# Sharing the PSUM banks on demand in an attention-plus-feed-forward kernel

## The chip, the cores and the metric

The kernel runs on one core of one Trainium2 chip. The metric is the device time in microseconds (us) of one execution. Before the change the median of four runs was 231.82 us (231.75 to 232.29).

The change has five parts: all eight PSUM banks are handed out on demand, singly or as pairs; both score blocks of a tile are computed in one run; two tiles are loaded at once on two queues; matmuls on zeros fill early idle time of TensorE; and the last output tile is finished in two column parts.

## The reference

Attention over 4 batches, 8 heads, 768 positions and head size 64 comes first, with a local window of 96 positions and 8 global positions. Its output, 3072 tokens of 512 values, goes through a feed-forward layer with 2048 hidden values.

```python
scores = scale * np.matmul(q, k.transpose(0, 1, 3, 2))
rel = pos[:, None] - pos[None, :]
keep = (pos[None, :] < n_global) | ((rel >= 0) & (rel < n_local))
scores = np.where(keep, scores + bias, -1e9)     # bias = -slope[head] * distance
a = softmax(scores)                              # cut: written out in the reference
x = np.matmul(a, v)  # -> (B*S, H*D)             # cut: heads put side by side
h = x @ w_in                                     # 512 -> 2048
out = (h - np.tanh(h)) @ w_out                   # 2048 -> 512
```

## The kernel before

The 3072 tokens are 24 tiles of 128. For each tile the kernel does the following:

1. It transposes k and q, computes the score block of its own 128 keys and the block of the previous 128 keys (S), takes the exponential (E), multiplies by a mask (M), multiplies by v (AV) and divides by the sum (R). The result x is transposed.
2. It projects x with `w_in` (m1). The result of 512 columns stands in one PSUM bank. ScalarE takes its tanh (th) and VectorE subtracts (g = h - tanh h). The bank is then free.
3. It multiplies g by `w_out` (m2) into one bank, which ScalarE copies out (ot) for the store.

From the fifth tile on, m1 takes two tiles at once. The first six tiles are transposed by TensorE, the later ones by DMA. A planner in the kernel's own Python simulates the engines with fixed durations. From that it decides the order of operations on each engine and which buffer each one gets. It puts no waits into the program: these are added when the program is built, from what each instruction reads and writes.

The kernel lays out PSUM as eight banks of 512 fp32 columns (its `BANK = 512`). Before the change they were split for good: two double banks for attention, four single ones for m1, m2 and the transposes.

```python
    bufs["pair"] = [psum.tile([P, 2, BANK], FP32, name=f"pair{i}") for i in range(2)]
    pl.pool("pair", 2)
    bufs["bank"] = [psum.tile([P, BANK], FP32, name=f"bank{i}") for i in range(4)]
    pl.pool("bank", 4)
    # ... cut ...
    def m1(g, f0):
        n, per = shape1(g)
        t = buf("bank", ("h", g, f0))
        xt = buf(xname(g), ("xT", g))
        for f in range(f0, f0 + per):
            j, fo = f // FJ, (f % FJ) * P
            for c in range(CD):
                nc.tensor.matmul(
                    t[:, (f - f0) * n : (f - f0 + 1) * n], w_in_bf[j][:, c, fo : fo + P], xt[:, c, 0:n],
                    start=(c == 0), stop=(c == CD - 1),
                )

    def m1_g(g, f0):
        t, th = buf("bank", ("h", g, f0)), buf("th", ("th", g, f0))
        # ... cut: g <- t - th, one VectorE instruction of 512 columns ...

    def m2(g, t, qq):
        o = buf("bank", ("o", u))
        # ... cut: four matmuls of 512 columns into o ...

    T_LD, T_W, T_ST, T_TR = 1.1, 3.15, 0.8, 0.7     # planned DMA times
    # ... cut ...
        for o in (0, 1) if i else (0,):
            pl.op(("S", u, o), PE, 0.24, lambda e, u=u, o=o: a_S(u, o),
                  # ... cut ...
                  take=[("pair", ("S", u, o)), ("po" if o else "pd", ("p", u, o))], mode="half")
            pl.op(("E", u, o), ACT, 0.97, lambda e, u=u, o=o: a_E(u, o), after=[("S", u, o)], give=[("S", u, o)])
```

`take` asks the planner for a buffer and `give` returns it. The operation `S` takes a double bank and `E` gives it back. `m1` takes a single bank and `g` gives it back.

The softmax here doesn't subtract the row's maximum and nothing guards it: scores larger than these inputs give would overflow.

## Time and profile before

The engines are PE (TensorE matmuls), PEld (its weight loads), DVE (VectorE), ACT (ScalarE), POOL (GpSimd) and SP. A profile names a group of instructions by its source line, and the lines moved with the change:

| what | before | after | its time in the profile before |
|---|---|---|---|
| score matmuls S | L282 | L317 | |
| projection m1, 8 matmuls of 256 columns | L340 | L375 | 0.87 us for 8 |
| tanh th (ACT) | L504 | L571 | 0.60 us |
| subtraction g (DVE) | L349 | L384 | 0.69 us |
| output matmuls m2, 4 of 512 columns | L359 | L418 | 0.86 us for 4 |
| copy of the output ot (ACT) | L270 | L305 | 0.58 us |

From the page of the kernel before, here are the span, the engine table, two rows of the 40 slices (busy tenths of TensorE, and its granted clock in tenths), the chain that ended last, and three groups. A group's columns are: count | busy us, mean ns of one | idle us before them, what ended most of it.

```profile
span 228.0 us, 5127 instructions
...
PE 207.8 (91%) x2056; PEld 143.3 (63%) x2056; DVE 128.1 (56%) x250; ACT 120.1 (53%) x192; POOL 71.4 (31%) x96
...
PE   1669699789999589999999999999999999999993
...
PEclk9999999999999959999999999999999999999999
...
PE 87%; DMA 4%; DVE 3%; POOL 2%; ACT 1%; issue 1%; POOLq 0%
PE bank L340 39%; PE bank L359 36%; PE pair L282 5%; PE pair L300 3%; DMA xT<-x 2%; PE pair L302 2%; PE bank L327 2%; DMA qb<-in_q_dram 2%; DVE x L312 1%; DVE pd L291 1%; ACT pd L286 0%; ACT po L286 0%; POOL vb L423 0%; POOL kb L423 0%; DVE xT L272 0%
...
L340 PE MATMUL bank<-xT,w_in_bf 128*128 128x256 bf16 (+1 forms) x896 | 100.1, 263 | 0.2 <-DMA xT<-x 0.2
L359 PE MATMUL bank<-w_out_bf,g 128*128 128x512 bf16 x384 | 95.2, 379 | 0.0
L349 DVE TENSOR_TENSOR g<-bank,th 128x512 bf16<-128x512 f32 x96 | 65.4, 689 | 50.5 <-ACT th L504 50.4
...
```

TensorE is busy 91% of the span and makes up 87% of the chain, so it is the bound. The `0.2` and `0.0` behind the two feed-forward groups say that TensorE almost never stood idle just before a feed-forward matmul. The idle time lies elsewhere. The stretches view gives it by time. Its columns are the stretch and its length, then busy us and instruction count of PE, PEld, DVE, ACT and POOL, then the granted clock, the DMA share and GB/s.

```profile
...
core 0: us, PE busy (x) PEld busy (x) DVE busy (x) ACT busy (x) POOL busy (x), PEclk, DMA share, GB/s
...
21.00:25.00 4.00, 2.00 (x42) 1.72 (x40) 2.91 (x5) 2.11 (x3) 1.41 (x2) 1.00 1.25 205
...
42.00:49.00 7.00, 4.80 (x54) 2.55 (x53) 3.83 (x8) 2.10 (x3) 4.66 (x6) 1.00 2.30 148
...
75.00:81.00 6.00, 2.83 (x48) 1.99 (x48) 4.19 (x11) 3.25 (x5) 3.50 (x4) 0.81 1.34 135
81.00:87.00 6.00, 5.94 (x47) 4.44 (x47) 2.94 (x5) 2.66 (x4) 1.69 (x2) 0.62 1.14 111
87.00:215.00 128.00, 128.00 (x1207) 88.22 (x1205) 78.39 (x142) 73.21 (x109) 21.96 (x26) 1.00 0.90 99
...
```

Up to 87 us there are holes: 2 us of 4 idle at 21 to 25, 2.2 of 7 at 42 to 49, and 3.2 of 6 at 75 to 81, after which the clock is lower. From 87 to 215 us TensorE is busy 128.00 of 128.00 us. What a piece of steady work costs shows in the chain of waits (start us, us, what):

```profile
...
204.49 0.87 PE bank L340 x8
205.37 0.86 PE bank L359 x4
206.23 0.87 PE bank L340 x8
...
```

### The profile page before, as it was taken

Reading aid. Unit: us, or ns where it says so; the run is one execution under the profiler, and the core shown is the slowest. Engines: PE = TensorE matmul, PEld = TensorE weight load, DVE = VectorE, ACT = ScalarE, POOL = GpSimd, SP = SyncE. Lnnn points to the kernel's source line nnn. Section 1 sums busy time; section 2 is a strip of 40 time slices with the busy share of each in tenths; the row PEclk is TensorE's granted clock in tenths of the full one; section 3 lists DMA queues with packets and bytes.
Section 4 is the critical chain, followed back from the end, with each engine's and each line's share of the span. In section 5 each row is a group of like instructions: output and inputs, shape, how many; then the busy total and the mean of one; then the engine's idle time right before and its main releaser. Section 6 shows DMA issues by size and latency. Waiting matters only on the chain.

```text
span 228.0 us, 5127 instructions
## 1 busy us (share of the span) xinstructions
PE 207.8 (91%) x2056; PEld 143.3 (63%) x2056; DVE 128.1 (56%) x250; ACT 120.1 (53%) x192; POOL 71.4 (31%) x96
## 2 busy tenths in 40 slices
PE   1669699789999589999999999999999999999993
PEld 0449698444864368676676676776667676666641
DVE  2565788530585748977675665576567553443310
ACT  5348466421676456666566466557546645443421
POOL 8996456531833514454314421400000000000000
PEclk9999999999999959999999999999999999999999
DMA  5999999999999999999999999793422321001112
GB/s 101 131 162 201 184 196 195 164 144 220 164 172 145 169 135 90 103 154 152 155 108 167 154 129 141 105 128 71 118 70 53 64 69 47 32 15 49 47 46 92
DMA packets 111959, 27.60 MB, mean 121 GB/s; under 512 B 104768, under 2 KB 108864, under 8 KB 111936
## 3 DMA queue, kind: packets, MB, share of 16 engines
q0 software_dynamic: 77024, 13.37, 83.5%
q1 hardware_dynamic: 34912, 13.90, 31.8%
q8 instruction: 16, 0.26, 0.5%
q14 instruction: 7, 0.06, 0.1%
HBM read 27.26 MB, written 6.29 MB: 147 GB/s over the span
## 4 chain that ended last, share of the span: by engine, by line
PE 87%; DMA 4%; DVE 3%; POOL 2%; ACT 1%; issue 1%; POOLq 0%
PE bank L340 39%; PE bank L359 36%; PE pair L282 5%; PE pair L300 3%; DMA xT<-x 2%; PE pair L302 2%; PE bank L327 2%; DMA qb<-in_q_dram 2%; DVE x L312 1%; DVE pd L291 1%; ACT pd L286 0%; ACT po L286 0%; POOL vb L423 0%; POOL kb L423 0%; DVE xT L272 0%
## 5 line engine op out<-in xcount | busy, mean ns | idle before, releaser
L340 PE MATMUL bank<-xT,w_in_bf 128*128 128x256 bf16 (+1 forms) x896 | 100.1, 263 | 0.2 <-DMA xT<-x 0.2
L359 PE MATMUL bank<-w_out_bf,g 128*128 128x512 bf16 x384 | 95.2, 379 | 0.0
L349 DVE TENSOR_TENSOR g<-bank,th 128x512 bf16<-128x512 f32 x96 | 65.4, 689 | 50.5 <-ACT th L504 50.4
L340 PEld LDWEIGHTS <-w_in_bf 128*128 128x128 bf16 x896 | 77.7, 101 | 18.8 <-issue 0.4
L504 ACT ACTIVATE th<-bank 128x512 f32<-128x512 f32 x96 | 56.9, 600 | 59.1 <-PE bank L340 58.9
L359 PEld LDWEIGHTS <-g 128*128 128x128 bf16 x384 | 36.4, 98 | 29.8
L423 POOL DMA_DIRECT2D kb<-in_k_dram x23 | 20.6, 894 | 50.9 <-DMA qT<-qb 24.9
L286 ACT ACTIVATE pd<-pair 128x1024 bf16<-128x1024 f32 x24 | 24.5, 1022 | 18.0 <-PE pair L282 17.9
L423 POOL DMA_DIRECT2D vb<-in_v_dram x24 | 21.5, 897 | 11.1 <-PE pair L282 5.1
L270 ACT COPY ot<-bank 128x512 f32<-128x512 f32 x24 | 14.0, 585 | 19.6 <-PE bank L359 19.6
L423 POOL DMA_DIRECT2D qb<-in_q_dram x23 | 20.4, 886 | 12.5 <-DMA qT<-qb 5.9
L291 DVE TENSOR_TENSOR pd<-pd,mk 128x1024 bf16<-128x1024 bf16 x24 | 16.6, 691 | 12.6 <-ACT pd L286 12.5
L286 ACT ACTIVATE po<-pair 128x1024 bf16<-128x1024 f32 x20 | 20.4, 1022 | 1.3 <-PE pair L282 1.1
L300 PE MATMUL pair<-vb,pd 128*128 128x65 bf16 x192 | 15.0, 200 | 4.6 <-DVE pd L291 4.5
L282 PE MATMUL pair<-qT,kT 64*128 64x128 bf16 x352 | 16.3, 227 | 2.4 <-DVE x L312 1.3
L300 PEld LDWEIGHTS <-pd 128*128 128x128 bf16 x192 | 12.9, 101 | 7.9 <-DVE pd L291 6.2
L282 PEld LDWEIGHTS <-kT 64*128 64x128 bf16 x352 | 10.9, 98 | 10.4 <-issue 9.4
L291 DVE TENSOR_TENSOR po<-po,mk 128x1024 bf16<-128x1024 bf16 x20 | 13.8, 692 | 6.0 <-ACT po L286 6.0
L312 DVE TENSOR_TENSOR x<-pair,rden 128x512 bf16<-128x512 f32 x24 | 16.6, 692 | 0.8
L302 PE MATMUL pair<-vb,po 128*128 128x65 bf16 x160 | 12.5, 194 | 1.6 <-DVE po L291 1.6
L302 PEld LDWEIGHTS <-po 128*128 128x128 bf16 x160 | 10.4, 97 | 3.5 <-DVE po L291 1.8
L327 PE MATMUL bank<-ident,kb 128*128 128x128 bf16 x24 | 3.3, 280 | 5.2 <-DVE kb L272 4.7
(29 smaller groups left out, 51.4 us busy)
## 6 DMA issues: line engine op xcount, KB each, us to landing
out_dram<-ot SPq DMA_DIRECT2D x24, 256.0 KB, 2.2
vb<-in_v_dram POOLq DMA_DIRECT2D x24, 128.0 KB, 6.2
kb<-in_k_dram POOLq DMA_DIRECT2D x23, 128.0 KB, 5.4
qb<-in_q_dram POOLq DMA_DIRECT2D x23, 128.0 KB, 6.0
w_in_bf<-in_moe_w_in_dram POOLq DMA_DIRECT2D x4, 512.0 KB, 10.4
w_out_bf<-in_moe_w_out_dram POOLq DMA_DIRECT2D x4, 512.0 KB, 12.9
kT<-kb SPq DMA_TRANSPOSE x18, 4.4
qT<-qb SPq DMA_TRANSPOSE x18, 4.0
```

What stands on the lines that cost most here:

```text
L270: nc.scalar.copy(out=dst, in_=src)
L282: nc.tensor.matmul(t[:, slot(2 * p + hh), :], kt[r, p, :], qt[r, p, :], start=True, stop=True)
L286: nc.scalar.activation(buf("po" if o else "pd", ("p", u, o)), t, AF.Exp, bias=0.0, scale=scale)
L291: nc.vector.tensor_tensor(out=p, in0=p, in1=mk[:, m, :, :], op=ALU.mult)
L300: nc.tensor.matmul(o, pd[:, slot(h), :], vd[:, h, :], start=True, stop=w is None)
L302: nc.tensor.matmul(o, buf("po", ("p", u, 1))[:, slot(h), :], bufs[vname(w)][got["vb", w]][:, h, :], start=False, stop=True,)
L312: nc.vector.tensor_tensor(out=x, in0=t[:, :, :, 0:Dh], in1=rd.to_broadcast([P, 2, NP, Dh]), op=ALU.mult,)
L340: nc.tensor.matmul(t[:, (f - f0) * n : (f - f0 + 1) * n], w_in_bf[j][:, c, fo : fo + P], xt[:, c, 0:n], start=(c == 0), stop=(c == CD - 1),)
L349: nc.vector.tensor_tensor(out=dst, in0=t.rearrange("q (b n) -> q b n", n=n), in1=th.rearrange("q (b n) -> q b n", n=n), op=ALU.subtract,)
L359: nc.tensor.matmul(o, gg[:, f, t * P : (t + 1) * P], w_out_bf[f // FJ][:, f % FJ, :], start=(f == 0), stop=(f == CF - 1),)
L423: pl.op(key, POOL, 0.75, lambda e, u=u, src=src, dst=dst: nc.gpsimd.dma_start(out=dst(), in_=rows(src, u)), after=[prev and ("issue", prev ...
L504: pl.op(("th", g, f), ACT, 0.55, lambda e, g=g, f=f: nc.scalar.activation(buf("th", ("th", g, f)), buf("bank", ("h", g, f)), AF.Tanh, bias ...
```

## The change

The intent: with a fixed split, attention may hold only two double banks, even when single banks are free. If any neighbouring free pair can serve as a double bank and any free bank as a single one, attention can run ahead of the feed-forward part, and both score blocks can be computed together. The other parts shorten the start and the end. The diff, cut to its core:

```diff
+    zeros = cpool.tile([P, 2 * P], BF16, name="zeros")
-    bufs["pair"] = [psum.tile([P, 2, BANK], FP32, name=f"pair{i}") for i in range(2)]
-    pl.pool("pair", 2)
-    bufs["bank"] = [psum.tile([P, BANK], FP32, name=f"bank{i}") for i in range(4)]
-    pl.pool("bank", 4)
+    pairs = [psum.tile([P, 2, BANK], FP32, name=f"pair{i}") for i in range(4)]
+    bufs["pair"] = {2 * i: t for i, t in enumerate(pairs)}
+    bufs["bank"] = [pairs[i // 2][:, i % 2, :] for i in range(8)]
 # ... in the planner; a bank in use has the time "never" (infinity) ...
+        def pick(size, free_banks, now):
+            best = None
+            if size == 2:
+                for i in range(0, 8, 2):
+                    t = max(free_banks[i], free_banks[i + 1])
+                    c = (max(t, now), -t, i)
+                    best = c if best is None or c < best else best
+            else:
+                for i in range(8):
+                    t = free_banks[i]
+                    c = (max(t, now), -max(t, free_banks[i ^ 1]), i)
+                    best = c if best is None or c < best else best
+            return best
 # ... loads, planned DMA times, masks ...
-    hw_loads = {0}
+    hw_loads = {0, 1}
-    T_LD, T_W, T_ST, T_TR = 1.1, 3.15, 0.8, 0.7
+    T_LD, T_W, T_ST, T_TR = 0.87, 2.4, 0.7, 0.5
+    DIST_AFTER = [("ld", "v", 1), ("in", 0), ("in", 1)]   # mask builds issued behind these
-                pl.op(("T", nm, u), SP, 0.6,               # DMA transposes, also those of x
+                pl.op(("T", nm, u), SP, 1.25,
 # ... scores ...
-            pl.op(("S", u, o), PE, 0.24, lambda e, u=u, o=o: a_S(u, o),
+        pl.op(("S", u), PE, 0.24 * len(os_), lambda e, u=u, os_=os_: [a_S(u, o) for o in os_],
+              take=[("pair", ("S", u, o)) for o in os_] + ...
 # ... zeros ...
+    def warm(e=None):
+        nc.tensor.matmul(buf("bank", "warm")[:, 0 : 2 * P], zeros[:, 0:P], zeros, start=True, stop=True)
+            if eng is PE and last is not None and "warm" in tags:
+                for _ in range(int((t - last - 0.15) / (0.22 if last < 8.0 else 0.15))):
+                    warm()
 # ... last tile in columns 0 to 383 and 384 to 511: m2_cols, ev_cols, store_cols, cut ...
```

A single bank is now one half of a two-bank tile. And `pick` sorts single banks by the *negative* of the time at which the bank beside them comes free. Of the banks free now, it therefore prefers one whose neighbour is in use, to keep whole pairs free for the scores.

More of the change, by code (lines that the diff above doesn't have):

```diff
@@ L39, in run @@
         avail = {n: [(0.0, i) for i in range(c)] for n, c in self.pools.items()}
+        banks = [0.0] * 8
         held = {}
@@ L48, in run @@
         order = []
+        never = float("inf")
+        def pick(size, free_banks, now):
[11 more added lines that the diff above has]
+            return best
         def ready(key):
@@ L53, in ready @@
             for a in o["after"]:
-                if a[0] == "issue":
-                    d = start.get(a[1])
-                else:
-                    d = done.get(a)
+                d = start.get(a[1]) if a[0] == "issue" else done.get(a)
                 if d is None:
@@ L60, in ready @@
                 t = max(t, d)
-            for p in o["take"]:
-                if not avail[p[0]]:
-                    return None
-                t = max(t, min(avail[p[0]])[0])
+            fb = None
+            for name, _ in o["take"]:
+                if name in ("bank", "pair"):
+                    fb = list(banks) if fb is None else fb
+                    size = 2 if name == "pair" else 1
+                    c = pick(size, fb, t)
+                    if c[0] == never:
+                        return None
+                    t = max(t, c[0])
+                    for i in range(c[2], c[2] + size):
+                        fb[i] = never
+                else:
+                    if not avail[name]:
+                        return None
+                    t = max(t, min(avail[name])[0])
             return t
@@ L88, in run @@
                     f"{k} {[a for a in ops[k]['after'] if (start.get(a[1]) if a[0] == 'issue' else done.get(a)) is None]}"
-                    f"{[p for p, _ in ops[k]['take'] if not avail[p]]}" for k in todo))
+                    f"{[p for p, _ in ops[k]['take'] if p in avail and not avail[p]]}" for k in todo))
             _, key, t, eng, us = best
@@ L92, in run @@
             end = t + us
+            if eng is PE:
+                end += 0.1 if mode and o["mode"] != mode else 0.0
+                mode = o["mode"]
             free[eng] = end
             start[key] = t
-            if eng is PE:
-                end += 0.1 if mode and o["mode"] != mode else 0.0
-                free[eng] = end
-                mode = o["mode"]
             if o["dma"]:
-                d0 = max(dma_free, end + (1.0 if eng is SP else 1.3))
+                d0 = max(dma_free, end + 1.2)
                 dma_free = d0 + o["dma"]
@@ L107, in run @@
             got = {}
+            now = t
             for name, tag in o["take"]:
-                b = min(avail[name])
-                avail[name].remove(b)
-                held[tag] = (name, b[1])
+                if name in ("bank", "pair"):
+                    size = 2 if name == "pair" else 1
+                    i = pick(size, banks, now)[2]
+                    for x in range(i, i + size):
+                        banks[x] = never
+                    held[tag] = (name, i)
+                else:
+                    b = min(avail[name])
+                    avail[name].remove(b)
+                    held[tag] = (name, b[1])
             for tag in o["give"]:
                 name, i = held.pop(tag)
-                avail[name].append((done[key], i))
+                if name in ("bank", "pair"):
+                    for x in range(i, i + (2 if name == "pair" else 1)):
+                        banks[x] = done[key]
+                else:
+                    avail[name].append((done[key], i))
                 got[tag] = i
-            for tag in list(held):
+            for tag in held:
                 got[tag] = held[tag][1]
@@ L185 @@
     w_out_bf = [cpool.tile([P, FJ, DM], BF16, name=f"w_out_bf{j}") for j in range(WJ)]
-    sb("kf", [P, H, Dh], FP32, 2)
+    sb("kf", [P, H, Dh], FP32, 4)
     sb("kb", [P, H * Dh], BF16, 4)
@@ L352, in m1_g, with m2_cols, ev_cols, store_cols @@
         )
+    SPLIT = 384
+    def m2_cols(u, part, qs):
+        g = group_of[u]
+        t = groups[g].index(u)
+        c0, c1 = (0, SPLIT) if part == 0 else (SPLIT, DM)
+        o = buf("bank", ("o", u, part))
+        gg = buf(gname(g), ("g", g))
+        for f in qs:
+            nc.tensor.matmul(
+                o[:, 0 : c1 - c0], gg[:, f, t * P : (t + 1) * P], w_out_bf[f // FJ][:, f % FJ, c0:c1],
+                start=(f == 0), stop=(f == CF - 1),
+            )
+    def ev_cols(e, u, part):
+        c0, c1 = (0, SPLIT) if part == 0 else (SPLIT, DM)
+        copy(e, buf("ot", ("ot", u))[:, c0:c1], buf("bank", ("o", u, part))[:, 0 : c1 - c0])
+    def store_cols(u, part):
+        b, i = tiles[u]
+        r = (b * NQ + i) * P
+        c0, c1 = (0, SPLIT) if part == 0 else (SPLIT, DM)
+        nc.sync.dma_start(out=out[r : r + P, c0:c1], in_=buf("ot", ("ot", u))[:, c0:c1])
     def m2(g, t, qq):
@@ L383 @@
     for m in range(3):
-        pl.op(("dist", m), POOL, 2.0 if m == 0 else 1.2, lambda e, m=m: build_dist(m), pri=-2 if m == 0 else 1)
+        pl.op(("dist", m), POOL, 2.0 if m == 0 else 1.2, lambda e, m=m: build_dist(m),
+              after=[("issue", DIST_AFTER[m])], pri=-2 if m == 0 else -1.5)
         for half in range(2):
@@ L418 @@
                           take=[("kf", ("kf", nm, u))], dma=T_LD)
-                    pl.op(key, DVE, 0.43, lambda e, u=u, nm=nm, dst=dst: copy(e, dst(), buf("kf", ("kf", nm, u))),
+                    pl.op(key, [(DVE, 0.43), (ACT, 0.6)], None,
+                          lambda e, u=u, nm=nm, dst=dst: copy(e, dst(), buf("kf", ("kf", nm, u))),
                           after=[("ldf", nm, u)], take=take, give=[("kf", nm, u)])
@@ L422 @@
                     go = [kk for a, kk in prog if a <= u - AHEAD - 1.5] if u >= 6 else []
-                    pl.op(key, POOL, 0.75, lambda e, u=u, src=src, dst=dst: nc.gpsimd.dma_start(out=dst(), in_=rows(src, u)),
+                    pl.op(key, POOL, 0.88, lambda e, u=u, src=src, dst=dst: nc.gpsimd.dma_start(out=dst(), in_=rows(src, u)),
                           after=[prev and ("issue", prev), go[-1] if go else None], take=take, dma=T_LD,
@@ L452 @@
         Te = (lambda nm, u: ("Te", nm, u) if u < NPE else ("T", nm, u))
-        for o in (0, 1) if i else (0,):
-            pl.op(("S", u, o), PE, 0.24, lambda e, u=u, o=o: a_S(u, o),
-                  after=[Te("k", u), Te("q", u), ("K", w) if o and tiles[w][1] else None, go,
-                         ("issue", ("S", u, 0)) if o else None],
-                  take=[("pair", ("S", u, o)), ("po" if o else "pd", ("p", u, o))],
-                  give=([("qT", u)] if o == (1 if i else 0) else []) + ([("kT", w)] if o and tiles[w][1] else []), mode="half")
-            pl.op(("E", u, o), ACT, 0.97, lambda e, u=u, o=o: a_E(u, o), after=[("S", u, o)], give=[("S", u, o)])
+        os_ = (0, 1) if i else (0,)
+        pl.op(("S", u), PE, 0.24 * len(os_), lambda e, u=u, os_=os_: [a_S(u, o) for o in os_],
+              after=[Te("k", u), Te("q", u), ("K", w) if i >= 2 else None, go],
+              take=[("pair", ("S", u, o)) for o in os_] + [("po" if o else "pd", ("p", u, o)) for o in os_],
+              give=[("qT", u)] + ([("kT", w)] if i >= 2 else []) + ([("kT", u)] if i == NQ - 1 else []), mode="half")
+        for o in os_:
+            pl.op(("E", u, o), ACT, 0.97, lambda e, u=u, o=o: a_E(u, o),
+                  after=[("S", u), ("issue", ("E", u, 0)) if o else None], give=[("S", u, o)])
             pl.op(("M", u, o), DVE, 0.7, lambda e, u=u, o=o: a_M(u, o),
                   after=[("E", u, o)] + [("mk", 2 if o else min(i, 1), half) for half in range(2)])
-        if i == NQ - 1:
-            pl.ops["S", u, 0]["give"].append(("kT", u))
         if 1 <= i < NQ - 1:
-            pl.op(("K", u), DVE, 0.2, lambda e, u=u: a_K(u), after=[("S", u, 0)])
+            pl.op(("K", u), DVE, 0.2, lambda e, u=u: a_K(u), after=[("S", u)])
             pl.op(("V", u), DVE, 0.25, lambda e, u=u: a_V(u), after=[("AV", u), ("ld", "v", b)])
@@ L488 @@
         else:
-            pl.op(("X", u), SP, 0.6,
+            pl.op(("X", u), SP, 1.25,
                   lambda e, u=u, g=g, off=off: nc.sync.dma_start_transpose(
@@ L492 @@
                   after=[("R", u), ("issue", prevx) if prevx else None], take=xt, give=[("x", u)], dma=T_TR, lag=0.5, pri=-1)
+    def warm(e=None):
+        nc.tensor.matmul(buf("bank", "warm")[:, 0 : 2 * P], zeros[:, 0:P], zeros, start=True, stop=True)
+    pl.op(("zero",), DVE, 0.1, lambda e: nc.vector.memset(zeros, 0.0), pri=-4)
+    pl.op(("warm",), PE, 0.2, warm, after=[("zero",)], take=[("bank", "warm")], pri=-4, mode="full")
+    pl.ops["S", HEAD - 1]["give"].append("warm")
     pl.op(("vone",), DVE, 0.6, lambda e: [nc.vector.memset(t[:, :, Dh : Dh + 1], 1.0) for t in bufs["vb"] + bufs["vb0_"]], pri=-3)
@@ L509 @@
         for t, u in enumerate(us):
+            if u == NU - 1:
+                for qq in range(4):
+                    pl.op(("m2", g, t, qq), PE, 0.65,
+                          lambda e, u=u, qq=qq: m2_cols(u, 0, range(qq * 4, qq * 4 + 4)),
+                          after=[("out", qq), ("g", g, (4 * qq + 3) // per * per)],
+                          take=[("bank", ("o", u, 0)), ("bank", ("o", u, 1)), ("acc", ("acc", u))] if qq == 0 else [],
+                          pri=2, mode="full")
+                pl.op(("m2", g, t, 4), PE, 0.9, lambda e, u=u: m2_cols(u, 1, range(CF)), after=[("issue", ("m2", g, t, 3))],
+                      give=[("g", g), ("acc", u)], pri=2, mode="full")
+                for part in range(2):
+                    pl.op(("ev", u, part), [(ACT, 0.45 if part == 0 else 0.25), (DVE, 0.5 if part == 0 else 0.26)], None,
+                          lambda e, u=u, part=part: ev_cols(e, u, part), after=[("m2", g, t, 3 + part)],
+                          take=[("ot", ("ot", u))] if part == 0 else [], give=[("o", u, part)], pri=1)
+                    pl.op(("st", u, part), SP, 0.4, lambda e, u=u, part=part: store_cols(u, part),
+                          after=[("ev", u, part)], give=[("ot", u)] if part else [], dma=0.5 if part == 0 else 0.3)
+                continue
             for qq in range(4):
@@ L520 @@
         [kk for a, kk in prog if kk[1] >= HEAD],
-        [("m2", g, t, qq) for g, us in enumerate(groups) for t in range(len(us)) for qq in range(4) if g >= HEAD],
+        [("m2", g, t, qq) for g, us in enumerate(groups) for t in range(len(us)) for qq in range(4) if g >= HEAD]
+        + [("m2", len(groups) - 1, 1, 4)],
     ]
@@ L532 @@
     with tc.manual_schedule(engines={PE, ACT, DVE, POOL, SP}):
+        last = None
         for t, n, key, eng, tags, end in sorted(order, key=lambda x: (x[0], x[1])):
             got = tags
+            if eng is PE and last is not None and "warm" in tags:
+                for _ in range(int((t - last - 0.15) / (0.22 if last < 8.0 else 0.15))):
+                    warm()
             pl.ops[key]["fn"](eng)
+            if eng is PE:
+                last = end
 _INS = ['q', 'k', 'v', 'n_global', 'n_local', 'moe_w_in', 'moe_w_out']
```

## The prediction

> **What bounds the kernel now.** TensorE: 207.8 of 228.0 us busy (engine table), 87% of the chain of waits. In the stretches view it is busy 128.0 of 128.0 us from 87 to 215 us, where a tile costs 8.09 us (its period in the chain). The change removes almost no TensorE work, so what can be won lies before 87 us and in the tail:
>
> - Head: the first input-projection matmul starts at 17.1 us (timeline).
> - Cold clock: until about 20.6 us a 128-column matmul takes 107 ns, later 56 ns (timeline). [...] The page's clock row does not show this start.
> - 21–25 us: TensorE idle 2.0 of 4.0 us, behind a tanh, exp and mask.
> - 42–49 us: idle 2.2 of 7; the chain shows 5.6 us there with only four output matmuls inside.
> - 75–81 us: the next projection waits 5.5 us for the DMA transpose of x. TensorE idles 3.2 us, the clock falls to half (stretches: 0.81, then 0.62), and 24 matmuls of 256 columns take 4.95 instead of 2.6 us. Together about 7.5 us.
> - Tail: last matmul 224.4, copy of 512 columns 0.58 us, store, end 228.0.
>
> The work at full rate adds up to about 197 us; some 31 us is head, stalls and tail.
>
> **What the change does.**
> 1. Zero matmuls from about 1.5 us: full clock at 5–8 us instead of 20.6. The first three projection groups lose their cold 1.7 us; about ten chain steps of 0.61 us become 0.40, mostly on the chain: 2–3.5 us in all.
> 2. Loads at once: the first POOL load is issued at about 1.4 us instead of 3.2, tile 1's k and q leave the POOL queue. DMA is over 90% busy from 6 to 75 us, so the gain is the earlier start, about 2 us, not more bandwidth.
> 3. Masks 1 and 2 earlier: the 3.3 us of mask exps at 17.1 no longer stand before the first tanh: 1–2 us of the 21–25 us stall.
> 4. PSUM pairs on demand and both score blocks in one run: four score-size slots instead of two, so attention runs ahead. With the plan's DMA-transpose issue at 1.25 us (trace: 1.2; it said 0.6), x transposes should be placed earlier. I expect the 75–81 us stall, and its half clock, mostly gone: 4–7 us; 1–2 us more from 42–49. Each separate score block costs 0.1 us of mode switch (chain: 0.97 against 0.86 for the next four matmuls): 0.5–1 us before 103 us (later they already stand together).
> 5. Last tile split 384+128: a last copy of about 0.26 us (estimate from 0.58 at 512 and 1.02 at 1024 columns) and a smaller store: 0.3–0.5 us.
>
> Sum 11–17 us; I take 13.5, since stalls partly reappear elsewhere.
>
> **Prediction: 218.3 us, range 212.5–225.5.** Faster by over 2%: 0.91; within 2%: 0.07; slower: 0.02.
>
> **Right if:** matmuls are at 56 ns before 9 us; the first projection starts at 13.5–16 us; no half-clock stretch after the start; TensorE still 100% busy in the last 120 us at 8.09 us a tile; last matmul to end about 3.1 us.
>
> **Wrong if:** the plan's shorter DMA times (0.87 for 1.1, 2.4 for 3.15) make in-order TensorE wait for weights at 20–45 us; if another wait for x or qT over 3 us cools the clock again; if sharing all eight banks, newest-freed first, makes steady-state matmuls wait on evictions (TensorE under 98% busy there); or if score runs needing two free pairs stall.

The 5 to 8 us of step 1 and the 3 us of the "wrong if" list are estimates. Measured in the clock records: full rate from 20.7 us before, from 12.2 us in the kernel after and from 7.0 us, not for good, in experiment 2; and before, at 78.7 us, a fall to half after 3.42 us in which TensorE was busy 1.07 us.

## More of the kernel before

Eight projection matmuls and four output matmuls alternate, 1.74 us for the two, with nothing between. The subtraction on VectorE runs beside them, and the waits view (waiting engine, line <- what it waited for: total us, times, longest) shows just one partner for it:

```profile
...
engine line waited for: us in total, times, longest us
DVE g L349 <- ACT th L504: 50.4, 60, 9.8
...
```

Remember this line: before the change, the subtraction waited for the tanh of its own bank and for nothing else.

## The result

The kernel after takes 258.75 us, median of its runs (258.25 to 259.0). The ratio to before is 1.1154 (95% interval 1.1132 to 1.1176). A ratio here is the mean time of one kernel's fast runs over that of the other's fast runs of the same rounds, so it is not quite the ratio of the medians. The change made the kernel 11.5% slower where 6% faster was expected.

The same rows of the page, for the kernel after:

```profile
span 257.2 us, 5222 instructions
...
PE 215.1 (84%) x2080; PEld 145.4 (57%) x2106; DVE 126.2 (49%) x250; ACT 119.8 (47%) x196; POOL 70.0 (27%) x94
...
PE   6777876989789859999889889889889886886864
...
PEclk9999999999999999999999999999999999999999
...
PE 66%; ACT 15%; DVE 9%; issue 6%; DMA 3%; SPq 0%; DVEq 0%; ACTq 0%
PE pair L418 30%; PE pair L375 29%; ACT th L571 12%; DVE g L384 7%; DMA kf<-in_k_dram 3%; ACT ot L305 2%; PE pair L362 2%; PE pair L398 1%; PE pair L317 1%; PE pair L335 1%; PE pair L556 1%; PE pair L337 1%; DVE x L347 0%; ACT xT L305 0%; SPq L478 0%
...
L375 PE MATMUL pair<-xT,w_in_bf 128*128 128x256 bf16 (+1 forms) x896 | 98.0, 257 | 13.8 <-ACT th L571 8.6
L418 PE MATMUL pair<-w_out_bf,g 128*128 128x512 bf16 x342 | 89.6, 378 | 18.6 <-ACT th L571 7.7
L384 DVE TENSOR_TENSOR g<-pair,th 128x512 bf16<-128x512 f32 x96 | 65.6, 689 | 79.9 <-PE pair L418 29.6
...
```

The durations did not change: a tanh, a subtraction and an output matmul take what they took (689 against 689 ns for the subtraction, 378 against 379 ns for the output matmul). What changed is the last column. TensorE idles 13.8 us before projection matmuls and 18.6 us before output matmuls, where it was 0.2 and 0.0, and the largest single part of it was ended by a tanh (8.6 and 7.7 us). TensorE's share of the chain fell from 87% to 66%, while tanh and subtraction entered with 12% and 7%. TensorE's busy time grew by 7.3 us (215.1 - 207.8), about what the zeros take (7.5 us for 34 matmuls), and its idle time from 20.2 to 42.1 us. This trace lacks 26 output matmuls (342 of 368 are recorded, while all 368 weight loads are), so its busy time is somewhat too low and its idle time too high, by an estimated 6 us at most (26 times the 0.22 us of one in the chain).

The stretches show that the steady part is worse, and the end more so:

```profile
...
87.00:215.00 128.00, 113.30 (x1051) 75.81 (x1067) 68.50 (x127) 63.37 (x95) 23.79 (x27) 1.00 0.90 96
215.00:257.20 42.20, 29.78 (x186) 17.54 (x187) 8.99 (x13) 10.54 (x19) 0.00 (x0) 1.00 0.10 38
...
```

TensorE is now busy 113.30 of the 128 us in which it never rested before, and 29.78 of the last 42.20. The first row spans the same stretch of time as the last row shown of before. Here is a piece of the chain near the end, where no attention is left and only the feed-forward part runs:

```profile
...
211.53 1.05 PE pair L375 x8
...
212.67 0.70 DVE g L384
...
213.40 0.61 ACT th L571
...
214.05 1.05 PE pair L375 x8
...
```

The three engines take turns. The matmuls finish (1.05 us), then the subtraction runs (0.70), then a tanh (0.61), then the next eight matmuls. One such round takes 2.52 us, from 211.53 to 214.05; what is not in these three is short gaps of issue. The four output matmuls of the round run beside the subtraction and the tanh, off the chain. Before, a round was 1.74 us, with the four output matmuls on the chain. It is odd that the subtraction comes *before* the tanh. Within one bank it comes after, so the chain must hop between banks.

The waits of VectorE and of TensorE say what waits for what:

```profile
...
DVE g L384 <- PE pair L418: 29.6, 23, 3.7
DVE g L384 <- ACT th L571: 23.8, 28, 2.5
DVE g L384 <- PE pair L375: 23.6, 13, 3.4
...
```

```profile
...
PE pair L375 <- ACT th L571: 8.6, 13, 1.3
PE pair L418 <- ACT th L571: 7.7, 12, 0.7
PE pair L418 <- DVE g L384: 5.5, 9, 0.9
...
```

The subtraction now waits 29.6 us for output matmuls and 23.6 us for projection matmuls. TensorE waits for tanhs and subtractions, which it did not do before. One of these waits rules out a simple explanation, that banks are handed out again too early. The last reader of a projection's bank is the subtraction, so a matmul that is to *reuse* such a bank waits for a subtraction. A matmul waiting for a *tanh* (8.6 + 7.7 us) cannot be waiting for that.

The loss grows over the whole run. The start times of output copies tell how far the kernel has come:

| start of the output copy, us | before | after |
|---|---|---|
| 1st tile | 49.41 | 50.50 |
| 7th tile | 101.66 | 104.56 |
| 17th tile | 183.21 | 198.76 |
| 24th tile (last) | 224.46 | 254.12 |

### Theories

- **A, the tile:** the waits put into the program are kept per PSUM tile, not per bank. Two unrelated results in the halves of one two-bank tile wait for each other, and the choice of neighbouring banks puts unrelated results together on purpose.
- **B, the order:** the new plan has a worse order of operations, or reuses banks too early. This would be there with any kind of tile.
- **C, another part of the change:** the score blocks in one run, the zeros or the shorter planned times cost the time.
- **D, the bank:** two engines slow each other down in neighbouring banks, whatever the tiles. The unchanged durations already speak against it (a subtraction takes 689 ns before and after, a tanh 600 and 599 ns, an output matmul 379 and 378 ns).

The expectations quoted below use the letters A, B and C in this sense. They do not name D.

The built programs speak for A. This is the same subtraction, from the list of instructions of the kernel after and of one with eight separate bank tiles and the same plan (experiment 2):

```
TensorTensor g_141<-pair_149,th_138 128x512 [waits PE_49,Activation_49]
TensorTensor g_141<-bank_149,th_138 128x512 [waits Activation_49]
```

The first has a wait on TensorE beside the one on the tanh. Of 96 subtractions, 46 wait for TensorE in the kernel after, 0 in the kernel before, 21 in experiment 1, 1 in experiment 2 and 4 in experiment 6. (The semaphores in the traces give the same numbers; the 40 in the expectation of experiment 6 was an earlier, lower count.) Of the 46, 44 wait for a matmul that writes the *other* bank of the tile. The feed-forward matmuls of the kernel after have 42 waits for a tanh, and in all 42 that tanh reads the other bank.

### The profile page after: what moved, and what is told of

Same layout as the page of the kernel before. It is cut to its first block, busy times and chain, and to the rows that moved or that the text cites. A ratio compares the mean times of both kernels' runs of the same rounds, so it can differ in the third digit from the quotient of the medians.

```text
span 257.2 us, 5222 instructions
## 1 busy us (share of the span) xinstructions
PE 215.1 (84%) x2080; PEld 145.4 (57%) x2106; DVE 126.2 (49%) x250; ACT 119.8 (47%) x196; POOL 70.0 (27%) x94
## 4 chain that ended last, share of the span: by engine, by line
PE 66%; ACT 15%; DVE 9%; issue 6%; DMA 3%; SPq 0%; DVEq 0%; ACTq 0%
PE pair L418 30%; PE pair L375 29%; ACT th L571 12%; DVE g L384 7%; DMA kf<-in_k_dram 3%; ACT ot L305 2%; PE pair L362 2%; PE pair L398 1%; PE pair L317 1%; PE pair L335 1%; PE pair L556 1%; PE pair L337 1%; DVE x L347 0%; ACT xT L305 0%; SPq L478 0%
## 5 line engine op out<-in xcount | busy, mean ns | idle before, releaser
L375 PE MATMUL pair<-xT,w_in_bf 128*128 128x256 bf16 (+1 forms) x896 | 98.0, 257 | 13.8 <-ACT th L571 8.6
L418 PE MATMUL pair<-w_out_bf,g 128*128 128x512 bf16 x342 | 89.6, 378 | 18.6 <-ACT th L571 7.7
L384 DVE TENSOR_TENSOR g<-pair,th 128x512 bf16<-128x512 f32 x96 | 65.6, 689 | 79.9 <-PE pair L418 29.6
L375 PEld LDWEIGHTS <-w_in_bf 128*128 128x128 bf16 x896 | 76.6, 98 | 36.9 <-issue 13.7
L571 ACT ACTIVATE th<-pair 128x512 f32<-128x512 f32 x96 | 56.6, 599 | 84.5 <-PE pair L375 45.0
L418 PEld LDWEIGHTS <-g 128*128 128x128 bf16 x368 | 35.2, 97 | 51.4 <-issue 22.3
L485 POOL DMA_DIRECT2D kb<-in_k_dram x22 | 19.6, 891 | 47.5 <-DMA kT<-kb 26.5
L305 ACT COPY ot<-pair 128x512 f32<-128x512 f32 (+2 forms) x25 | 14.2, 570 | 35.7 <-PE pair L375 16.0
L317 PE MATMUL pair<-qT,kT 64*128 64x128 bf16 x352 | 14.2, 219 | 0.0
L353 DVE COPY kT<-kT 128x32 bf16<-128x32 bf16 x16 | 4.1, 256 | 14.8 <-PE pair L317 14.8
```

Of the source, the lines that this page charges most:

```text
L305: nc.scalar.copy(out=dst, in_=src)
L317: nc.tensor.matmul(t[:, slot(2 * p + hh), :], kt[r, p, :], qt[r, p, :], start=True, stop=True)
L375: nc.tensor.matmul(t[:, (f - f0) * n : (f - f0 + 1) * n], w_in_bf[j][:, c, fo : fo + P], xt[:, c, 0:n], start=(c == 0), stop=(c == CD - 1),)
L384: nc.vector.tensor_tensor(out=dst, in0=t.rearrange("q (b n) -> q b n", n=n), in1=th.rearrange("q (b n) -> q b n", n=n), op=ALU.subtract,)
L418: nc.tensor.matmul(o, gg[:, f, t * P : (t + 1) * P], w_out_bf[f // FJ][:, f % FJ, :], start=(f == 0), stop=(f == CF - 1),)
L485: pl.op(key, POOL, 0.88, lambda e, u=u, src=src, dst=dst: nc.gpsimd.dma_start(out=dst(), in_=rows(src, u)), after=[prev and ("issue", prev ...
```

## The experiments

Twelve kernels ran, in three batches on three chips. Each batch ran the kernel before too, and its median there was 230.7, 229.8 and 230.75 us. Comparisons between batches go through the ratio to before. All outputs were correct. The medians are over all runs; one run of experiment 3 and one of experiment 5 fell in the slow state, and the ratios leave them out.

| run | what | median us | ratio to before, 95% |
|---|---|---|---|
| after | the change | 258.75 | 1.1154 (1.1132–1.1176) |
| 1 | before, four single banks as halves of two tiles | 264.67 | 1.1485 (1.1434–1.1535) |
| 2 | after, eight tiles of one bank | 223.19 | 0.9682 (0.9644–0.9720) |
| 3 | after, fixed split, separate tiles | 229.59 | 0.9928 (0.9858–0.9999) |
| 4 | as 3, score blocks separate | 227.33 | 0.9854 (0.9813–0.9894) |
| 5 | as 2, no filling with zeros | 225.70 | 0.9784 (0.9726–0.9841) |
| 6 | after, the choice of bank reversed | 224.89 | 0.9776 (0.9725–0.9827) |
| 7 | as 2, later planned landing of DMA transposes | 222.90 | 0.9684 (0.9634–0.9735) |
| 8 | as 2, planned DMA times of before | 227.77 | 0.9897 (0.9832–0.9962) |
| 9 | as 2, 8 tiles transposed by TensorE | 221.22 | 0.9589 (0.9526–0.9652) |
| 10 | as 2, 10 tiles transposed by TensorE | 221.06 | 0.9569 (0.9516–0.9622) |
| 11 | as 2, score blocks separate | 227.30 | 0.9849 (0.9776–0.9922) |
| 12 | as 2, loads and masks of before | 225.95 | 0.9793 (0.9735–0.9850) |

### Experiment 1: only the joined tiles, in the kernel before

```diff
-    bufs["bank"] = [psum.tile([P, BANK], FP32, name=f"bank{i}") for i in range(4)]
+    joined = [psum.tile([P, 2, BANK], FP32, name=f"joined{i}") for i in range(2)]
+    bufs["bank"] = [joined[i // 2][:, i % 2, :] for i in range(4)]
```

The planner sees nothing of this edit: order and banks stay the same.

> The kernel before with one edit: its four single PSUM banks are drawn as halves of two tiles of two banks. Plan, instruction order and bank numbers stay. Theory A (the slowdown is waits between the two halves of one PSUM tile, put in because dependencies are kept per tile): slower by 8 to 35 us (240 to 267), TensorE no longer 100% busy after 87 us, matmuls waiting for tanh. Rival B (newest-freed bank policy) and rival C (another part of the change): 231 to 233, no such waits.

Measured: 264.67 us, ratio 1.1485. One line about how the same banks are declared costs 34 us (264.67 - 230.7), more than the whole change. Theory B cannot explain this, since the order is that of before. In TensorE's waits, things appear that had no place there:

```profile
...
PE joined L341 <- ACT ot L271: 10.7, 10, 1.2
...
PE joined L360 <- DVE g L350: 5.1, 11, 0.5
...
```

A projection now waits 10.7 us for copies of the output, and output matmuls wait 5.1 us for subtractions. In the built program, 10 of the 11 waits of projections for an output copy, and all 33 waits of output matmuls for a subtraction, are for one that reads the bank beside their own.

### Experiment 2: the whole change, with eight tiles of one bank

```diff
-    pairs = [psum.tile([P, 2, BANK], FP32, name=f"pair{i}") for i in range(4)]
-    bufs["pair"] = {2 * i: t for i, t in enumerate(pairs)}
-    bufs["bank"] = [pairs[i // 2][:, i % 2, :] for i in range(8)]
+    bufs["bank"] = [psum.tile([P, BANK], FP32, name=f"bank{i}") for i in range(8)]
+    bufs["pair"] = {i: bufs["bank"][i : i + 2] for i in range(0, 8, 2)}
 # ... cut: S, E, AV and R address the two tiles of a pair ...
```

A pair is now two tiles, so the instructions that spanned both banks are split: the exponential into two of 512 columns (about 0.60 us each for one of 1.02), the reciprocal and the division likewise. Plan and banks are those of the kernel after.

> The changed kernel with eight separate one-bank PSUM tiles; a pair is two of them, so exp and normalise run in two halves of 512 columns. Same plan and same bank for each piece of work. Theory A: 212 to 226, TensorE over 97% busy from 100 to 200 us, no matmul waiting for a tanh. Rival B (reusing the newest-freed bank, packed next to an occupied one): still over 245. Rival C: still over 245.

Measured: 223.19 us, ratio 0.9682. Against the 258.75 us of the kernel after, the repair is worth about 34 us (the ratios 1.1154 and 0.9682 of some 231 us), although ScalarE and VectorE have more to do (122.5 us busy for 119.8, and 132.0 for 126.2). In its stretches, TensorE is again at its bound in the steady part:

```profile
...
60.00:75.00 15.00, 10.13 (x113) 5.71 (x112) 9.15 (x22) 8.67 (x18) 5.24 (x6) 0.90 1.83 160
...
100.00:200.00 100.00, 99.59 (x930) 67.99 (x928) 60.73 (x124) 56.67 (x104) 15.74 (x18) 1.00 0.91 99
...
```

Theories B and D fall as explanations of the loss, since the order and the banks in use are unchanged: all 96 subtractions read the same bank in both built programs. Theory C falls too, since every other part of the change is still there. With tiles of one bank the waits are kept by bank, and the outputs were correct. Keeping them by pairs of banks cost 258.75 against 223.19 us here.

The first row shows a stretch that stays bad: from 60 to 75 us TensorE is busy 10.13 of 15. Its longest wait lies there:

```profile
...
PE bank L316 <- DMA qT<-qb: 5.3, 2, 4.9
...
```

Two score matmuls wait 5.3 us in all for the DMA transpose of q. The stall that stood at 75 to 81 us before did not go: it moved to 67 to 72 us and has another operand.

### Experiments 3 and 4: a fixed split, with everything else of the change

Experiment 3 takes pairs only from banks 0 to 3 (two double tiles) and singles only from 4 to 7 (four own tiles), oldest-freed first:

```diff
-                for i in range(0, 8, 2):
+                for i in (0, 2):
-                for i in range(8):
+                for i in range(4, 8):
-                    c = (max(t, now), -max(t, free_banks[i ^ 1]), i)
+                    c = (max(t, now), t, i)
 # ... cut: the same turn of the sign for pairs, and the tiles ...
```

> The changed kernel with the fixed PSUM split of before (two pairs, four banks, a tile each), everything else as changed. Theory A and rival B both: 213 to 226. Rival C (score blocks in one run, zero matmuls or plan constants cost the time): over 240.

Experiment 4 also computes the score blocks separately, as before:

```diff
-        pl.op(("S", u), PE, 0.24 * len(os_), lambda e, u=u, os_=os_: [a_S(u, o) for o in os_],
+        for o in os_:
+            pl.op(("S", u, o), PE, 0.24, lambda e, u=u, o=o: a_S(u, o),
 # ... cut: what each waits for, takes and gives ...
```

> As e3, and the two score blocks separate again as before: only early loads, zero matmuls, plan constants and the split last tile remain. Theory A: 213 to 225; beside e3 it tells what the one run of score blocks costs with only two pairs: I expect e3 slower by 0 to 3 us. Rival C in its form 'one run of score blocks': e3 over 240 and this one under 226; in its form 'zeros or constants': both over 240.

Measured: 0.9928 and 0.9854, or 229.59 and 227.33 us. Both lie far under the 240 us of rival C, and both miss the 213 to 226 and 213 to 225 told for theory A: without sharing, the change gains less than expected. With two double tiles, joining the score blocks looks 0.7% slower, but the intervals overlap, so a cost is not shown. Both are slower than experiment 2: sharing the banks and joining the blocks is worth 1.7% over neither (0.9854 against 0.9682).

### Experiment 5: no filling with zeros

```diff
-                for _ in range(int((t - last - 0.15) / (0.22 if last < 8.0 else 0.15))):
-                    warm()
+                pass
```

> e2 without the zero matmuls that fill gaps of the head (the first one stays); plan and order else the same. If the zeros bring what I predicted for them (2 to 3.5 us): 225 to 227 against about 223 for e2, and full clock some 4 to 8 us later than in e2 (there at 13.6 us). If they bring nothing: within 0.7 us of e2.

Measured: 0.9784 against 0.9682, which is 1.0% or about 2.3 us. The two ran on different chips and the intervals lie only just apart. In the clock record of the trace, full rate comes at 19.9 us here, as before (20.7), and at 7.0 us in experiment 2. But there it fell back to half from 10.5 to 13.9 us, and again from 71.9 to 75.3 us, although TensorE was working. The stretches of experiment 2 around both:

```profile
...
7.04:10.46 3.42, 1.60 (x22) 1.09 (x23) 1.94 (x4) 2.06 (x6) 3.28 (x7) 1.00 2.02 171
10.46:13.87 3.41, 3.41 (x40) 2.68 (x39) 2.40 (x8) 2.90 (x10) 3.39 (x5) 0.50 1.46 183
68.48:71.89 3.41, 0.00 (x0) 0.00 (x0) 0.49 (x2) 0.00 (x0) 1.30 (x2) 1.00 1.93 124
71.89:75.31 3.42, 3.00 (x21) 1.54 (x22) 1.57 (x3) 2.06 (x4) 0.87 (x1) 0.50 1.77 198
...
```

The second and the fourth row are the half-clock stretches (0.50). The rows ahead of them are the 3.41 us before. Ahead of the second drop TensorE did nothing. Ahead of the first it was busy 1.60 of 3.42 us, and its longest gap was 1.01 us. So the clock fell after a stretch with no gap over 1.01 us, at 47% busy. Another drop followed 1.07 busy of 3.42 us (before, 75.3 to 78.7).

The 13 traces of fast runs together say more. In each, the changes of the clock lie whole multiples of 3.41 us apart, and the half-clock stretches that ended again lasted 3.41 or 6.83 us. Cut at these boundaries, up to the last matmul, they hold 787 stretches at full clock: after all 20 with at most 1.60 us of TensorE busy the clock fell, and after all 767 others, with at least 1.80 us, it stayed. The longest gap does not separate them: one drop had none over 0.91 us (before, 75.3 to 78.7), and one stretch with a gap of 1.46 us kept its clock (before, 20.7 to 24.1). The way back took more: of 28 stretches at half clock, the 8 with at most 2.71 us busy were followed by another at half, and the 20 with at least 2.81 us by full clock. This is what these traces show, not a law.

### Experiment 6: two-bank tiles, the choice of bank reversed

```diff
-                    c = (max(t, now), -max(t, free_banks[i ^ 1]), i)
+                    c = (max(t, now), max(t, free_banks[i ^ 1]), i)
```

One sign: singles now prefer a bank whose neighbour is free and has been free longest.

> The changed kernel, two-bank tiles kept, with one sign turned in the choice of a bank: it takes the one whose neighbour has been free longest, instead of the one beside an occupied or newly freed bank. Theory A (waits between halves of a tile): built instructions show 4 of 96 subtractions that also wait for TensorE, against 40 of 96 in the changed kernel, so most of the loss goes: 222 to 238. If the packing has no part in it: over 250.

Measured: 224.89 us, ratio 0.9776. The joined tiles stay, but in the built program only 4 of 96 subtractions wait for TensorE, and only 2 waits of feed-forward matmuls are for a tanh on the neighbouring bank (42 in the kernel after). Waits of projections for a subtraction on the neighbouring bank remain (34). In the chain, eight projection and four output matmuls follow each other without a gap again, at 0.87 and 0.86 us:

```profile
...
205.19 0.87 PE pair L375 x8
206.07 0.86 PE pair L418 x4
...
```

So most of the loss was the rule that packs neighbours, acting on joined tiles. It changes the order too, so by itself it would be weaker evidence than experiments 1 and 2. The packing rule is not needed for such a loss: experiment 1 lost 34 us with joined tiles and the old choice of banks.

### Experiment 7: are the DMA transposes placed too late in the plan?

```diff
-                      ... dma=T_TR, lag=0.5)            # k and q
+                      ... dma=T_TR, lag=3.0)
-                  ... dma=T_TR, lag=0.5, pri=-1)        # x
+                  ... dma=T_TR, lag=2.0, pri=-1)
```

> e2 with a later planned landing of the DMA transposes (q and k by 2.5 us, x by 1.5 us more), so that the plan puts the work that needs them later. In e2 TensorE waits 5.3 us for q transposes at 62 to 72 us and the clock then falls to half for 3.4 us. If the plan's too early landing is the cause: no such wait over 1.5 us, no half-clock stretch after the head, 216 to 221. If DMA is simply too slow for that stage: the wait turns up elsewhere and the time stays at 222 to 225.

Measured: 0.9684, equal to experiment 2 (0.9682). The wait for q is shorter, but still there, and the clock fell again (from 72.1 to 78.9 us):

```profile
...
PE bank L316 <- DMA qT<-qb: 3.6, 1, 3.6
...
```

My idea that the plan was only too hopeful about the landing of the transposes gets no support.

### Experiment 8: planned DMA times of before

```diff
-    T_LD, T_W, T_ST, T_TR = 0.87, 2.4, 0.7, 0.5
+    T_LD, T_W, T_ST, T_TR = 1.1, 3.15, 0.8, 0.7
```

> e2 with the plan's DMA times of before (1.1 us a load, 3.15 a weight block, 0.7 a transpose). The plan then puts work later; if its times are too long, TensorE idles less on DMA but runs late on the weights: 221 to 228. If the shorter times of the change had been the damage in e2, under 219.

Measured: 0.9897 against 0.9682, 2.2% or 5 us slower. The shorter times, which I had named as a risk, help. They steer the order alone, because no DMA is any faster for them.

### Experiments 9 and 10: fewer DMA transposes

```diff
-    NPE = 6
+    NPE = 8        # experiment 10: 10
```

> e2 with the q, k and x transposes of tiles 6 and 7 moved from the DMA to TensorE (8 tiles instead of 6). e7 left open whether DMA is too slow in the stretch from 60 to 75 us. If so, six DMA transposes fewer there shorten the TensorE wait for q (5.3 us in e2) and remove the half clock after it, for about 1.3 us of TensorE work (six transposes of 0.22): 216 to 221. If the stage is bound by loads alone: 222 to 225 with the wait still over 3 us.

> As e9 with 10 tiles: four tiles' transposes on TensorE, 2.6 us of work added. If the DMA transposes are the bottleneck of 60 to 75 us: no wait for a transpose over 1 us before 75 us, 215 to 221. Otherwise 223 to 226.

Measured: 0.9589 and 0.9569, medians 221.22 and 221.06 us, each just above the 221 us told. The wait for q fell from 5.3 us (6 tiles) to 1.6 (8) and 0.3 (10), and the clock record of experiment 10 shows no half rate from 17.1 us to the last matmul. The wait in experiment 10, and its stretch from 60 to 75 us, which is full:

```profile
...
PE bank L316 <- DMA qT<-qb: 0.3, 1, 0.3
...
60.00:75.00 15.00, 15.00 (x173) 11.91 (x171) 12.92 (x27) 10.44 (x20) 4.72 (x6) 1.00 1.60 133
...
```

Against the 10.13 us of experiment 2 this is the stall that I had expected the change to remove. What limited it was the DMA transposes. Each occupies the issuing engine SP for about 1.2 us and lands 4.0 to 5.5 us after issue (medians by operand: 4.0 to 4.4 us before, 4.3 to 5.5 in experiment 2), three of them per tile, at a time when loads fill the DMA (the DMA row of experiment 2 is at 9 tenths from about 6 to 150 us). A transpose on TensorE takes 0.22 us in the chain of the kernel before (and a copy out of PSUM), from a TensorE that would otherwise have waited. Experiment 10 is the fastest kernel here and beats both the kernel before and the kernel after. Its interval overlaps that of experiment 9, which in turn just overlaps that of experiment 2; that of experiment 10 lies just below experiment 2's.

### Experiment 11: single-bank tiles, separate score blocks

The edit is that of experiment 4, on experiment 2.

> e2 with the two score blocks as separate runs. I predicted 0.5 to 1 us for the one run: 223.5 to 224.5 here. If the one run costs, because it needs four banks at once, this one is faster than e2 by 1 us or more.

Measured: 0.9849, equal to experiment 4 (0.9854), which has the fixed split; the 227.30 us miss the 223.5 to 224.5 told. So no gain from handing out banks on demand by itself is seen. With both score blocks in one run it goes to 0.9682, 1.7% or 3.8 us better. A run of both blocks needs two double banks at once. With a fixed split that is all there are, which fits with joining not paying there.

### Experiment 12: loads and masks of before

```diff
-    hw_loads = {0, 1}
+    hw_loads = {0}
-              after=[("issue", DIST_AFTER[m])], pri=-2 if m == 0 else -1.5)
+              pri=-2 if m == 0 else 1)
```

> e2 with the loads as before: tile 1's k and q on the POOL queue, and the masks built by POOL ahead of the first load. I predicted about 2 us for the earlier loads and 1 to 2 us for the masks: 225 to 227. If they bring nothing: within 1 us of e2.

Measured: 0.9793 against 0.9682, 1.1% or about 2.6 us, on different chips and with intervals only just apart. Early loads and early masks are worth that much together.

## Why the prediction was wrong

The failed step is step 4, "PSUM pairs on demand and both score blocks in one run: four score-size slots instead of two, so attention runs ahead … I expect the 75–81 us stall, and its half clock, mostly gone: 4–7 us". Its sign was wrong. It counted the banks and left out a cost: waits between the two halves of one tile, which come from how the banks are declared.

- **What cost the time.** Single banks became halves of two-bank tiles. The built program then orders uses of one half against uses of the other, and the choice of bank puts unrelated results side by side on purpose. Experiment 1 shows the cost without the rest of the change (+34 us), experiment 2 shows the change without the cost (about -34 us), and experiment 6 removes most of it with one sign. The 2.52 us round of matmuls, subtraction and tanh is what it looks like in the chain.
- **The "wrong if" list came close.** It named that sharing banks, "newest-freed first, makes steady-state matmuls wait on evictions (TensorE under 98% busy there)". The symptom came (113.30 of 128 us, 89%). The mechanism is another one: not a bank used again too soon, but the neighbour of a bank in use. Waits of matmuls for a tanh show the difference. Another entry, "another wait for x or qT over 3 us cools the clock again", came true in experiment 2, where the longest wait for q was 4.9 us and the clock was at 0.50 from 71.9 to 75.3 us, but not in the kernel after.
- **The size was off even with the tiles repaired.** Experiment 2 gains 3.2%, about 7.4 us, not 13.5. The stall at 75 to 81 us did not go but came back at 67 to 72 us, on the transpose of q instead of x, with a half clock after it. Moving the planned landing did not change the time (experiment 7). With fewer DMA transposes the wait shrank to 1.6 and 0.3 us, and the half clock was gone (experiments 9 and 10).
- **Mode switch, 0.5 to 1 us** (the prediction's name for the extra 0.11 us that the four output matmuls just after a score block take in the chain of before, 0.97 against 0.86 us; that it is a switch of mode is not shown): joining the score blocks is worth 3.8 us, but only with banks on demand (experiments 2 and 11). With a fixed split no gain is seen (3 and 4). By what share this is that 0.11 us and by what share the different plan is not shown.
- **Step 1, zeros, 2 to 3.5 us:** worth about 2.3 us (experiment 5). The clock did not behave as told: full at 12.2 us in the kernel after, not at 5 to 8, and in experiment 2 at 7.0 us but not for good.
- **Steps 2 and 3, loads and masks, 3 to 4 us together:** worth about 2.6 us (experiment 12), slightly under. The first projection began at 15.10 us in experiment 2, inside the range told, and at 16.53 us in the kernel after, outside it.
- **Step 5, tail, 0.3 to 0.5 us:** right. From the start of the last copy to the end it is 3.54 us before and 3.08 us after; the copy itself takes 0.27 us for 0.58.
- **The risk of shorter DMA times** did not come true: they help by 2.2% (experiment 8).
- **"No half clock after the start"** held for the kernel after, but there it shows nothing of the reason given, since the stall of before was gone in a run that was slower everywhere. It failed in experiment 2.

The parts taken away one at a time do not add up to the 7.4 us, since each removal also changes the plan. Two things stay open: by what mechanism shorter planned times help, and how much of experiment 6's remaining distance to experiment 2 (0.9776 against 0.9682, on different chips) is due to the remaining joint waits and how much to its different order.

## What to carry to other kernels

Declare memory in the unit in which it is reused: if two results are independent, give them separate tiles, and let an operation that needs both take two tiles, even if that splits an instruction in two. When a change touches how buffers are declared, compare the waits in the built instructions before asking how many buffers there are; a wait with a partner that never touches the same bank is the sign. When a stall is expected to go, name the resource that ends it: here it was the DMA transposes and not PSUM, so the stall only moved.
